# Sliding-window attention as banded dense scores, with a new layout of the projected memory tokens and later weight loads

## Chip, cores and metric

One core of one Trainium2 chip. The metric is the device time of one launch in microseconds (us). Times quoted are medians of several executions; all executions that are compared are in the fast state unless said otherwise (for the 16 runs of the kernel before that ran beside the changed one the record lists no states; the highest is 1.7% above the lowest). Stage times come from one profiled execution of each kernel.

## The reference, cut to what matters

The output is `g * a + (1 - g) * b` for 2048 tokens of width 640. `b` is a sliding attention: each token looks at 8 tokens, 2 apart, with 32 heads of width 20. `a` is a recurrent attention over 64 segments of 32 tokens; 8 memory tokens pass from one segment to the next.

```python
def _B_ref(x, wqkv, wo):
    B, S, D = x.shape
    H = 32
    W, dil = (8, 2)
    ...                                    # q, k, v = x @ wqkv, 32 heads of 20
    idx = pos[:, None] - off[None, :]      # off = 0, 2, 4 .. 14
    mask = idx >= 0
    logits = jnp.einsum('bhsd,bhswd->bhsw', q, kg) * scale
    logits = jnp.where(mask[None, None, :, :], logits, -1000000000.0)
    attn = _softmax(logits, axis=-1)
    o = jnp.einsum('bhsw,bhswd->bhsd', attn, vg)
    return (...) @ wo

def _A_ref(x, mem0, Wq, Wk, Wv, Wo, seg_len):
    for s in range(n_seg):                 # 64 segments, one after the other
        h = jnp.concatenate([mem, xs], axis=1)
        ...                                # q, k, v: 640 -> 32 heads of 192
        ...                                # causal attention within the segment
        o = jnp.einsum('bhte,hed->btd', o, Wo)
        mem = o[:, :M, :].copy()
        outs.append(o[:, M:, :])
```

## The kernel before

It has three stages, one after the other. *Part B* is the sliding attention. The *prepass* projects the last 8 tokens of every segment (512 tokens in all) to queries, keys and values and packs them by segment into a buffer in DRAM. *Part A* is the loop over segments; it reads that buffer and streams 22 of the 80 weight slices (384 KB each) again for each segment, while 58 stay in SBUF.

Part B before (cut): for each of the 8 window positions an elementwise product, summed over each head's 20 rows by a matmul with a 0/1 matrix; then the weights are spread back over the rows by a second 0/1 matmul, copied, multiplied by the shifted values, and summed by identity matmuls.

```python
for w in range(8):
    prod = wk.tile([128, KC, BT], BF, name="prod")
    eng = nc.vector if w % 2 == 0 else nc.gpsimd
    eng.tensor_tensor(out=prod[:], in0=qT[:], in1=kT[:, :, 14 - 2 * w:14 + BT - 2 * w], op=ALU.mult)
    ...                       # 20 head-sum matmuls
...                           # max, exp, sum, reciprocal, product
for c in range(KC):
    for wh in range(2):
        ...                   # 16 expansion matmuls into e_ps
        for sb in range(4):
            nc.scalar.copy(ae[:], e_ps[sb][:])
            eng = nc.vector if ei % 3 != 2 else nc.gpsimd
            eng.tensor_tensor(out=pv[:], in0=ae[:], in1=vwin, op=ALU.mult)
            ...               # 4 identity matmuls into o_ps
```

The prepass before (cut). `evac` copies PSUM to SBUF and takes its engine from a pattern: "a" is ScalarE, "d" is VectorE; here the pattern is "add", so VectorE gets two of three.

```python
k.evac_pat = "add"
...
k.part_b(); k.load_late(0); k.prepass(); k.load_late(1); k.part_a()

with tc.tile_pool(name="pre_zs", bufs=2) as zp:
    zT = zp.tile([128, KC, NZ], BF, name="zT", bufs=1)
    nc.scalar.dma_start(zT[:], self.zT_dram[:].rearrange("p c i s -> p c (i s)"))
    for mi, m in enumerate(("q", "k")):
        for R in range(4):
            ZS = zp.tile([128, nseg, 96], BF, name="ZS")
            sls = [self.get_slice((m, R, kc)) for kc in range(KC)]
            for j in range(4):
                for t in range(3):
                    ...       # 5 matmuls of 128x512 into ps
                    zc = ZS[:].rearrange("p s (c i) -> p i s c", i=8)[:, :, :, 4 * t + j] if m == "q" else \
                        ZS[:].rearrange("p s (i c) -> p i s c", i=8)[:, :, :, 4 * t + j]
                    self.evac(zc, ps[:].rearrange("p (i s) -> p i s", i=8))
            z0 = (768 if m == "q" else 0) + 96 * R
            nc.scalar.dma_start(self.zpk_dram[:, :, z0:z0 + 96].rearrange("s p f -> p s f"), ZS[:])
    ...                       # the value part: 16 groups of 15 matmuls, ZV, stores
```

Of the 58 slices that stay, 29 (values and output weights) are loaded late, 21 after part B and 8 after the prepass, because part B needs the room.

The softmax here doesn't subtract the row's maximum and nothing guards it: scores larger than these inputs give would overflow.

Of the kernel before, what the change touches and what calls it, by code (L numbers as in the profile page):

```python
# [8 lines left out]
ALU = mybir.AluOpType  # L9
# [5 lines left out]
NEG = -1.0e9  # L15

N_STREAM = 22
N_LATE = 29
N_LATE2 = 8
# [9 lines left out]
class _K:  # L29
# [26 lines left out]
    def pst(self, shape, dtype=F32, name="ps"):  # L56
        shape = list(shape)
        assert shape[0] == 128
        nfree = 1
        for d in shape[1:]:  # L60
            nfree *= d
        tot = 2048 // mybir.dt.size(dtype)
        assert nfree <= tot
        t = self.psum.tile([128, tot], dtype, tag="ps", name=name)
        v = t[:, 0:nfree]
        if len(shape) > 2:
            names = "abcdef"[:len(shape) - 1]
            v = v.rearrange("p (%s) -> p %s" % (" ".join(names), " ".join(names)), **dict(zip(names, shape[1:])))
        return v

    def warm(self, n):
        n = int(round(n * _DEV.get("warm", 0)))
        if n <= 0:
            return
        pf = self.pst([128, 128], F32, name="ps_warm")
        for i in range(n):
            self.nc.tensor.matmul(pf[:], lhsT=self.ident[:], rhs=self.ident[:], start=True, stop=True,
                                  skip_group_check=True)
# [21 lines left out]
    def build_consts_b(self, const):  # L100
        nc = self.nc
        ones = const.tile([128, 640], BF, name="ones")
        nc.vector.memset(ones[:], 1.0)
        KC = self.KC
        eh = const.tile([128, KC, 32], BF, name="ehead")
        nc.gpsimd.affine_select(out=eh[:], in_=ones[:, 0:KC * 32].rearrange("p (c h) -> p c h", c=KC),
                                pattern=[[128, KC], [-20, 32]], compare_op=ALU.is_ge, fill=0.0, base=0,
                                channel_multiplier=1)
        nc.gpsimd.affine_select(out=eh[:], in_=eh[:], pattern=[[-128, KC], [20, 32]], compare_op=ALU.is_ge,
                                fill=0.0, base=19, channel_multiplier=-1)  # L110
        self.ehead = eh
        eht = const.tile([128, 640], BF, name="eheadT")
        for sb in range(4):
            sl = slice(32 * sb, 32 * sb + 32)
            nc.gpsimd.affine_select(out=eht[sl, :], in_=ones[sl, :], pattern=[[1, 640]], compare_op=ALU.is_ge,
                                    fill=0.0, base=0, channel_multiplier=-20)
            nc.gpsimd.affine_select(out=eht[sl, :], in_=eht[sl, :], pattern=[[-1, 640]], compare_op=ALU.is_ge,
                                    fill=0.0, base=19, channel_multiplier=20)
        self.eheadT = eht

    def part_b(self):
        nc, tc, KC, S = self.nc, self.tc, self.KC, self.S
        BT = _DEV.get("BT", 512)
        SBT = BT // 4
        NTB = BT // 128
        NB = S // BT
        scale_b = 20.0 ** (-0.5)
        self.bsc_dram = self.dram.tile([S, 640], BF, name="bsc_dram")
        self.zT_dram = self.dram.tile([128, KC, 8, S // 32], BF, name="zT_dram")
# [3 lines left out]
        with ExitStack() as ctx:  # L133
            wpool = ctx.enter_context(tc.tile_pool(name="b_w", bufs=1))
            xin = ctx.enter_context(tc.tile_pool(name="b_xin", bufs=2))
            act = ctx.enter_context(tc.tile_pool(name="b_act", bufs=_DEV.get("b_act_bufs", 1)))
            wk = ctx.enter_context(tc.tile_pool(name="b_wk", bufs=_DEV.get("b_wk_bufs", 2)))
            sm = ctx.enter_context(tc.tile_pool(name="b_sm", bufs=_DEV.get("b_sm_bufs", 1)))
            self.build_consts_b(wpool)
            wqkv_sb = wpool.tile([128, KC, 1920], BF, name="wqkv_sb")  # L140
            nc.scalar.dma_start(wqkv_sb[:], self.wqkv.rearrange("(c p) f -> p c f", p=128))
            wo_sb = wpool.tile([128, KC, 640], BF, name="wo_sb")
            nc.scalar.dma_start(wo_sb[:], self.wo.rearrange("(c p) f -> p c f", p=128))
            gw_sb = wpool.tile([128, KC, 1], BF, name="gw_sb")
            nc.scalar.dma_start(gw_sb[:], self.gate_w.rearrange("(c p o) -> p c o", p=128, o=1))
            gz_sb = wpool.tile([128, self.NT], F32, name="gz_sb")
            halo_k = wpool.tile([128, KC, 14], BF, name="halo_k")
            halo_v = wpool.tile([128, KC, 14], BF, name="halo_v")
            nc.gpsimd.memset(halo_k[:], 0.0)
            nc.gpsimd.memset(halo_v[:], 0.0)  # L150

            for blk in range(NB):
                t0 = blk * BT
                xT = act.tile([128, KC, BT], BF, name="xT_blk")
                xs = []
                for i in range(NTB):
                    x_sb = xin.tile([128, 640], BF, name="x_sb")
                    nc.scalar.dma_start(x_sb[:], self.x2d[t0 + i * 128:t0 + (i + 1) * 128, :])
                    xs.append(x_sb)
                for kc in range(KC):  # L160
                    ps = self.pst([128, BT], BF, name="ps_xT")
                    for i in range(NTB):
                        nc.tensor.transpose(ps[:, i * 128:(i + 1) * 128], xs[i][:, kc * 128:(kc + 1) * 128],
                                            self.ident[:])
                    self.evac(xT[:, kc, :], ps[:])
                nsb = BT // 32
                xv = xT[:].rearrange("p c (s t) -> p s c t", t=32)
                xh = act.tile([128, nsb, KC, 32], BF, name="xh_blk")
                nc.gpsimd.tensor_copy(xh[:, :, :, 8:32], xv[:, :, :, 0:24])
                nc.gpsimd.tensor_copy(xh[:, :, :, 0:8], xv[:, :, :, 24:32])  # L170
                nc.gpsimd.dma_start(self.xh_dram[blk * nsb:(blk + 1) * nsb].rearrange("s p f -> p s f"),
                                    xh[:].rearrange("p s c t -> p s (c t)"))
                zx = act.tile([128, KC, 8, nsb], BF, name="zx_blk")
                nc.gpsimd.tensor_copy(zx[:].rearrange("p c i s -> p s c i"), xv[:, :, :, 24:32])
                nc.gpsimd.dma_start(self.zT_dram[:, :, :, blk * nsb:(blk + 1) * nsb].rearrange("p c i s -> p (c i) s"),
                                    zx[:].rearrange("p c i s -> p (c i) s"))
                ps_g = self.pst([128, NTB], F32, name="ps_g")
                for i in range(NTB):
                    for kc in range(KC):
                        nc.tensor.matmul(ps_g[:, i:i + 1], lhsT=xT[:, kc, i * 128:(i + 1) * 128],  # L180
                                         rhs=gw_sb[:, kc, :], start=(kc == 0), stop=(kc == KC - 1))
                gsl = slice(blk * NTB, (blk + 1) * NTB)
                nc.vector.tensor_copy(gz_sb[:, gsl], ps_g[:])
# [116 lines left out]
    def weights_setup(self):  # L300
# [20 lines left out]
        for k in rest:  # L321
            if k in self.late_keys:
                continue
# [458 lines left out]
```

## Time and profile before

| | before |
|---|---|
| median, all 16 runs beside the changed kernel | 2356.55 us (2335.93 to 2376.16) |
| part B ends, prepass starts (profiled run, span 2353.4) | 427 us |
| prepass: queries and keys / values | 161 / 55 us |
| hand-over to part A | 17 us |
| part A | 1693 us |

The stages are read from when tiles of one stage are first and last touched, and then from the busy time of all engines between those moments. The prediction below prints those rows. In a row the numbers are the stretch, its length, the busy time of each engine with its number of instructions, the granted TensorE clock, the mean busy share of the 16 DMA engines, and GB/s.

### The profile page before, as it was taken

What the parts mean: (1) busy time and instruction counts of PE and PEld (TensorE: products, weight loads), DVE (VectorE), ACT (ScalarE), POOL (GpSimd) and SP (SyncE); (2) the same over time, 40 slices, a digit from 0 to 9 for tenths busy, and PEclk for the clock granted to TensorE, in tenths of its full rate; (3) what the DMA queues carried; (4) which work ended last, traced back from release to release, by engine and by line L of the source; (5) the groups of instructions that cost most, each with busy time, mean ns of one, the idle gap of its engine ahead of it and who ended that gap; (6) DMA issues with size and microseconds to landing.
All of it is one profiled execution on the core that took longest, in us unless ns stands there. A gap on an engine that the chain in (4) does not pass through costs nothing.

```text
span 2353.4 us, 90790 instructions
## 1 busy us (share of the span) xinstructions
PE 1978.4 (84%) x40951; PEld 1135.8 (48%) x40951; DVE 944.9 (40%) x2148; ACT 784.0 (33%) x1807; POOL 211.4 (9%) x196
## 2 busy tenths in 40 slices
PE   3566575776979999999998999999999998899998
PEld 1334243322445555555555555555555555555555
DVE  2554545799423333333333333333333333333333
ACT  0314233455123333333333333333333333333333
POOL 4452544000010000000000000000000000000000
PEclk9575675899989999999999999999999999999999
DMA  8110010677699999999999999999999999999997
GB/s 309 48 40 23 15 32 1 210 101 114 173 326 344 334 326 370 345 365 328 364 333 347 345 348 359 330 363 329 360 341 339 356 344 345 327 358 349 355 343 294
DMA packets 329396, 649.09 MB, mean 276 GB/s; under 512 B 107280, under 2 KB 129744, under 8 KB 329008
## 3 DMA queue, kind: packets, MB, share of 16 engines
q1 hardware_dynamic: 221104, 583.23, 69.4%
q10 hardware_dynamic: 104720, 49.57, 8.8%
q0 software_dynamic: 3184, 10.49, 1.6%
q8 instruction: 320, 5.24, 0.8%
q14 instruction: 68, 0.56, 0.1%
HBM read 615.79 MB, written 29.36 MB: 274 GB/s over the span
## 4 chain that ended last, share of the span: by engine, by line
PE 51%; DMA 23%; DVE 9%; issue 8%; POOL 6%; ACT 3%; ACTq 0%; POOLq 0%; DVEq 0%; SPq 0%
PE ps_qk L490 14%; PE ps_wo L629 8%; DMA wst<-in_A_Wv_dram 7%; PE ps_v L567 6%; DMA wst<-in_A_Wk_dram 6%; DVE ZS L89 6%; PE ps_qkT L504 4%; DMA wst<-wscr 4%; POOL prod L213 3%; PE ps_oT L585 3%; PE ps_woz L629 2%; PE o_ps L259 2%; POOL pv L257 2%; DMA wst<-in_A_Wq_dram 2%; PE ps_S L521 2%
## 5 line engine op out<-in xcount | busy, mean ns | idle before, releaser
L495 ACT CAST QS<-ps_qk 128x384 bf16<-128x384 f32 x512 | 239.8, 479 | 485.8 <-PE ps_qk L490 465.4
L490 PEld LDWEIGHTS <-hT 128*32 128x32 bf16 x10240 | 239.6, 96 | 179.9 <-issue 40.1
L490 PE MATMUL ps_qk<-wst,hT 128*32 128x384 bf16 x2816 | 243.6, 334 | 21.1 <-DMA wst<-in_A_Wk_dram 15.9
L567 PE MATMUL ps_v<-wlate_v,hT 128*32 128x384 bf16 x3584 | 238.9, 331 | 1.3 <-issue 1.2
L629 PEld LDWEIGHTS <-ZQ 128*32 128x32 bf16 x6144 | 187.1, 100 | 109.2 <-issue 47.1
L490 PE MATMUL ps_qk<-wres_k,hT 128*32 128x384 bf16 x3584 | 227.4, 329 | 0.9 <-issue 0.8
L490 PE MATMUL ps_qk<-wres_q,hT 128*32 128x384 bf16 x3840 | 217.8, 331 | 7.5 <-issue 4.1
L504 PE MATMUL ps_qkT<-ident,QS 128*128 128x128 bf16 x1536 | 174.9, 223 | 29.8 <-ACT QS L495 29.8
L598 DVE CAST ZQ<-ps_oT 128x192 bf16<-128x192 f32 x256 | 79.6, 352 | 266.2 <-ACT ZQ L598 266.2
L507 DVE COPY ZQ<-ps_qkT 128x384 bf16<-128x384 bf16 x256 | 91.4, 357 | 212.8 <-PE ps_qkT L504 212.7
L504 PEld LDWEIGHTS <-QS 128*128 128x128 bf16 x1536 | 88.3, 98 | 176.2 <-issue 101.6
L567 PEld LDWEIGHTS <-hT 128*32 128x32 bf16 x5120 | 119.7, 96 | 101.5 <-issue 45.1
L89 DVE CAST ZS<-ps_pre 128x512 bf16<-128x512 f32 x64 | 163.6, 2984 | 9.5 <-PE ps_pre L373 9.5
L629 PE MATMUL ps_wo<-wst,ZQ 128*32 128x384 bf16 (+1 forms) x1408 | 153.0, 328 | 16.6 <-issue 9.2
L511 DVE COPY KV<-ps_qkT 128x384 bf16<-128x384 bf16 x256 | 91.6, 358 | 180.1 <-PE ps_qkT L504 180.1
L629 PE MATMUL ps_wo<-wlate_ob,ZQ 128*32 128x256 bf16 x2688 | 149.2, 285 | 9.2 <-issue 9.2
L567 PE MATMUL ps_v<-wst,hT 128*32 128x384 bf16 x1536 | 134.3, 333 | 24.1 <-DMA wst<-in_A_Wv_dram 21.2
L629 PE MATMUL ps_wo<-wlate_oa,ZQ 128*32 128x384 bf16 x2048 | 150.5, 347 | 4.6 <-issue 4.1
L717 POOL DMA_DIRECT2D out_dram<-a x16 | 8.7, 544 | 1606.6 <-DVE ZQ L507 1412.3
L598 ACT CAST ZQ<-ps_oT 128x192 bf16<-128x192 f32 x256 | 69.2, 322 | 233.6 <-PE ps_oT L592 233.6
L251 ACT CAST ae<-e_ps 128x512 bf16<-128x512 f32 x160 | 88.2, 588 | 74.7 <-PE e_ps L245 45.9
L259 PE MATMUL o_ps<-pv,ident 128*128 128x128 bf16 x640 | 90.0, 300 | 27.3 <-POOL pv L257 17.5
(145 smaller groups left out, 2688.9 us busy)
## 6 DMA issues: line engine op xcount, KB each, us to landing
wst<-in_A_Wk_dram SPq DMA_DIRECT2D x390, 384.0 KB, 5.5
wst<-in_A_Wv_dram SPq DMA_DIRECT2D x390, 384.0 KB, 5.7
wst<-in_A_Wq_dram SPq DMA_DIRECT2D x325, 384.0 KB, 5.6
wst<-wscr SPq DMA_DIRECT2D x320, 384.0 KB, 5.4
ZQ<-zpk_dram ACTq DMA_DIRECT2D x64, 288.0 KB, 5.7
zpk_dram<-ZS ACTq DMA_DIRECT2D x8, 1536.0 KB, 10.7
zpk_dram<-ZV ACTq DMA_DIRECT2D x32, 192.0 KB, 3.1
wres_q<-in_A_Wq_dram SPq DMA_DIRECT2D x15, 384.0 KB, 6.7
```

Of the source, the lines that this page charges most:

```text
L89: nc.vector.tensor_copy(out, in_)
L213: eng.tensor_tensor(out=prod[:], in0=qT[:], in1=kT[:, :, 14 - 2 * w:14 + BT - 2 * w], op=ALU.mult)
L251: nc.scalar.copy(ae[:], e_ps[sb][:])
L259: nc.tensor.matmul(o_ps[:, sb * SBT:(sb + 1) * SBT], lhsT=self.ident[:], rhs=pv[:, wi, :], start=first, stop=(wh == 1 and wi == 3), skip_g ...
L490: nc.tensor.matmul(pq[32 * j:32 * j + 32, 0:384], lhsT=hT[:, kc, :], rhs=sl[:, 384 * j:384 * j + 384], start=(kc == 0), stop=(kc == KC - 1 ...
L495: nc.scalar.copy(st, pq[:, 0:384])
L504: nc.tensor.transpose(pT[:, t, :, :, :].rearrange("p j b i -> p (j b i)"), st[:, 128 * t:128 * t + 128], self.ident[:])
L507: nc.vector.tensor_copy(QT[:, 1:5, 12 * R:12 * R + 12, :].rearrange("p b c i -> p c b i"), pT.rearrange("p t j b i -> p (t j) b i"))
L511: nc.vector.tensor_copy(KT[:, 12 * R:12 * R + 12, :].rearrange("p c k -> p (c k)"), pT.rearrange("p t j b i -> p (t j b i)"))
L567: nc.tensor.matmul(pv[32 * j:32 * j + 32, 0:384], lhsT=hT[:, kc, :], rhs=sl[:, 384 * j:384 * j + 384], start=(kc == 0), stop=(kc == KC - 1 ...
L598: cp(oTx[:, c0:c0 + 6, :], pos[j // 2][:, j % 2, 0:240].rearrange("p (c q) -> p c q", q=40)[:, :, 8:40])
L629: nc.tensor.matmul(pss[part][32 * jj:32 * jj + 32, 0:n], lhsT=oT[:, 24 * (R // 2) + 6 * j + 3 * (R % 2) + t, :], rhs=o_weights(part, c), s ...
```

## The change

The intent is to turn part B into dense matmuls, to make the prepass's scattered stores cheap, and to give part B the room for this by loading most weights after it. Four parts:

1. **Part B.** Even and odd tokens are two sequences, so the window is a band of 8 in each. Heads are padded from 20 to 32 rows. For each block of 484 tokens and group of 4 heads there are dense scores (128 keys by 121 queries), two exps and two products with a band mask (one for each pair of heads), value matmuls and ones matmuls for the sums, and 1/sum as exp(-ln).
2. **Late loads.** 55 of the 58 slices that stay are loaded late: 46 after part B (12 query, 14 key, 14 value, 6 output), 9 after the prepass.
3. **Layout.** In the prepass the segment is now the outer and the position in it the inner index. The query store writes runs of 8 bf16; the key store still steps 24 bytes per element.
4. **Split.** Evictions alternate between the two engines ("ad").

```diff
-N_LATE = 29
-N_LATE2 = 8
+N_LATE = 55
+N_LATE2 = 9
 ... part B rewritten (cut to the inner step)
+            def scores(b, g):
+                ...
+                for hp in range(2):
+                    ps = psS.tile([128, 2, 512], F32, tag="S", name="ps_bS")
+                    for u in range(nu):
+                        a = 242 * (u // 2) + u % 2
+                        for r in range(2):
+                            rs = slice(64 * hp + 32 * r, 64 * hp + 32 * r + 32)
+                            nc.tensor.matmul(ps[0:nk, r, nq * u:nq * u + nq], lhsT=kT[rs, a:a + 2 * nk - 1:2],
+                                             rhs=qT[rs, a:a + 2 * nq - 1:2], ...)
+                    nc.scalar.activation(Pv, ps[0:nk, :, 0:nq * nu], ACT.Exp, scale=scale_b)
+                    nc.vector.tensor_tensor(out=P4, in0=P4, in1=m.to_broadcast([nk, 2, nu, nq]), op=ALU.mult)
+            def values(b, g):
+                ...           # ones and value matmuls into pz and po, one bank each
+                nc.scalar.activation(rz[:, 0:nt], pz[:, 0:nt], ACT.Ln)
+                nc.scalar.activation(rz[:, 0:nt], rz[:, 0:nt], ACT.Exp, scale=-1.0)
+                nc.vector.tensor_tensor(out=dst, in0=po..., in1=rz..., op=ALU.mult)
 ... order of a step: next projection, scores, values of the step before, output tile
 ... late loads
-        self.late_keys = set(cand[len(cand) - N_LATE:])
+        first = ["q", "k", "v", "oa", "ob"]
+        self.late = sorted(rest, key=lambda k: first.index(k[0]))[-N_LATE:]
 ... prepass
-                            zc = ZS[:].rearrange("p s (c i) -> p i s c", i=8)[:, :, :, 4 * t + j] if m == "q" else \
-                                ZS[:].rearrange("p s (i c) -> p i s c", i=8)[:, :, :, 4 * t + j]
-                            self.evac(zc, ps[:].rearrange("p (i s) -> p i s", i=8))
+                            zc = ZS[:].rearrange("p s (c i) -> p s c i", i=8)[:, :, 4 * t + j, :] if m == "q" else \
+                                ZS[:].rearrange("p s (i c) -> p s c i", i=8)[:, :, 4 * t + j, :]
+                            self.evac(zc, ps[:].rearrange("p (s i) -> p s i", i=8))
 ... value stores: 4 instead of 2 per tile, half of them issued by GpSimd
-    k.evac_pat = "add"
+    k.evac_pat = "ad"
```

## The prediction

> **What bounds the kernel now.** The program has three stages that run one after the other: the sliding-window attention (part B), the projection of the segment-end tokens (the prepass), and the 64 segments of the recurrent attention (part A). I first asked for the lifetimes of the tiles that mark the borders. The first prepass matmul starts at 427 us, the last scattered-layout eviction ends near 590, the last prepass matmul near 643, and part A runs steadily from 660. Then I read the busy time of every engine in those stretches.
>
> ```profile
> core 0: us, PE busy (x) PEld busy (x) DVE busy (x) ACT busy (x) POOL busy (x), PEclk, DMA share, GB/s
> 0.00:37.00 37.00, 2.82 (x23) 2.01 (x23) 1.43 (x5) 2.07 (x3) 11.21 (x24) 1.00 0.92 340
> 130.00:226.00 96.00, 60.55 (x622) 35.59 (x620) 49.22 (x61) 30.51 (x55) 44.75 (x27) 0.63 0.10 22
> 421.00:427.00 6.00, 0.00 (x0) 0.00 (x0) 0.00 (x0) 0.00 (x0) 0.00 (x0) 0.74 0.69 243
> 427.00:588.00 161.00, 121.10 (x481) 49.08 (x482) 158.34 (x63) 84.73 (x32) 0.00 (x0) 0.92 0.75 144
> 588.00:643.00 55.00, 53.46 (x239) 23.57 (x238) 24.84 (x34) 8.90 (x16) 0.00 (x0) 0.97 0.63 165
> 643.00:660.00 17.00, 2.07 (x43) 1.21 (x43) 1.74 (x25) 1.43 (x3) 7.03 (x40) 0.68 0.83 247
> 660.00:2353.40 1693.40, 1554.18 (x37651) 916.76 (x37648) 560.61 (x1774) 562.75 (x1534) 16.93 (x32) 0.98 0.96 344
> ```
>
> The reader sees three things. One block of part B takes 96 us with no engine over 61 us busy and the matmul clock at 0.63: it is a chain of waits, not a full engine. The query and key half of the prepass takes 161 us with VectorE busy 158 of them. Part A takes 1693 us with DMA at 0.96 and PE at 0.92, and the change leaves it alone. So 72% of the span is out of reach.
>
> Next, the groups of part B and of the prepass, to name the links.
>
> ```profile
> L213 DVE TENSOR_TENSOR prod<-qT_blk,kT_ext x16: 1492/3838/5596, 51.6 to 356.5; 128x2560 bf16<-128x2560 bf16 x16
> L213 POOL TENSOR_TENSOR prod<-qT_blk,kT_ext x16: 4597/4874/5907, 53.2 to 361.1; 128x2560 bf16<-128x2560 bf16 x16
> L257 DVE TENSOR_TENSOR pv<-ae,vT_ext x108: 413/426/1317, 87.5 to 414.0; 128x512 bf16<-128x512 bf16 x108
> L87 ACT CAST qT_blk<-ps_qkv x7: 586/586/587, 41.8 to 336.3; 128x512 bf16<-128x512 f32 x7
> L89 DVE CAST kT_ext<-ps_qkv x14: 690/691/693, 46.1 to 341.6; 128x512 bf16<-128x512 f32 x14
> L89 DVE CAST ZS<-ps_pre x64: 2718/2984/3019, 429.7 to 590.3; 128x512 bf16<-128x512 f32 x64
> L87 ACT CAST ZS<-ps_pre x32: 2707/2726/3132, 432.3 to 584.4; 128x512 bf16<-128x512 f32 x32
> ```
>
> Columns after the colon are least, median and largest nanoseconds. The products of line 213 take turns on VectorE and GpSimd, 5 us apiece when they meet. The prepass eviction of 128x512 costs VectorE 2984 ns where the plain one costs 691, and ScalarE 2726 where the plain one costs 586: the same data, scattered into ZS.
>
> **What the Trainium skill says.** (1) "TensorE: Matmul & The Clock Gate", Part 1: an idle window of about 3.4 us brings the array to half rate. The trace agrees: 0.63 granted in part B's block with its 4 to 9 us gaps, 0.97 in the dense 588 to 643. (2) "SBUF — State Buffer", Door 1: lines of 16 bytes, and each access to a new line is penalised. The trace agrees: the scattered store steps 192 bytes per element and costs four times the plain one, while the query transposes' copy in part A, in runs of 8 bf16, takes the 358 ns of the contiguous key copy. (3) "VectorE: DVE Perf Modes", the tier table: tensor_tensor in bf16 has a double rate, and single with a PSUM operand. The trace agrees: 2560 elements in 1492 ns at best is 1.7 per ns. (4) "ScalarE: Activation LUTs", What ACT_TABLE_LOAD costs: 0.833 ns per element for every function; here 586 ns for 512 and 479 for 384 give 0.84 and a fixed 0.16 us. Exp and Ln share one loaded table, as before.
>
> **The change, part by part.**
>
> *Part B is rewritten.* It removes all elementwise products over eight window positions, the head-sum matmuls, the max, the head-expansion matmuls with their 160 ScalarE copies, and the identity-matmul sums. In their place even and odd tokens are separate sequences, in which the dilated window is a band of 8; per block of 484 tokens and group of 4 heads the kernel makes dense scores of 128 keys by 121 queries, one exp, a band mask, a value matmul and a ones matmul for the sums. There are 32 full steps (4 blocks, 8 groups) and 8 short ones of 112 tokens.
>
> PE per full step: projections are 10 matmuls of 484 and 498 columns. The old 128x512 matmul runs at 0.216 us in a stream (five in 1.08), so 10 x 0.207 = 2.07 us. Scores: 16 of 121 columns, two row tiles at once; the old expansion matmuls of 128 columns followed each other every 22 ns with four tiles, I take 30, so 0.5. Values and sums: 32 matmuls, the old head-sum ones did 20 in 0.46, so 0.6. Each change of tile shape left 0.2 us of idle before; three give 0.6. Sum 3.8, times 32 is 121. Short steps: 8 x 1.8 = 14. Output tiles: 16 x 16 matmuls of 320 columns at 0.135 = 34. Values projection: 18 x 10 x 0.135 = 24. Transposes and gate: 4 x 2 = 8. PE total 201 us at full clock.
>
> ScalarE per full step: key eviction 0.575, two exps over 968 elements 2 x 0.97, Ln 0.56, Exp 0.60: 3.7, times 32 is 118. Short steps 10, its half of the value, transpose and output evictions 21: 149. VectorE: query eviction 0.66, final product from PSUM 0.66, two masks at 0.65 (double rate) to 1.16 (single): 2.6 to 3.6, so 84 to 116, plus about 35 of the rest: 120 to 150. GpSimd nearly leaves the path.
>
> So PE bounds part B. It won't be full: the projection, value, transpose and output groups share two PSUM banks, and ScalarE's in-order queue puts an eviction behind exps of 1 us. I add about 15% for this: 230. Before the first projection, x, the weights (3.3 MB at some 310 GB/s) and the padded copies take about 15 us, where the old kernel had its first projection at 37. Part B thus ends near 245 instead of 421: minus 176.
>
> *Weights.* Only 3 resident slices now load during part B, and 55 late: 46 after it, 9 after the prepass (21 and 8 before). 46 x 393 KB at 344 GB/s is 53 us, but they arrive in order of use, and five slices feed 13 us of matmuls, while their load takes 5.7. Three of the first five are already there and one is streamed. I keep 4 us of gap for the 6 before: minus 2.
>
> *Prepass.* With the segment outside and the position inside, the query store writes runs of 8 bf16 (16 bytes), so it falls to the plain 0.6 to 0.7 us and PE bounds it: 240 x 0.216 = 52, say 54. The key store still steps 24 bytes per element, a new line each time. I keep the old cost of about 2.6 us, but shared equally by two engines now: 24 x 2.7 = 65. The value half is PE-bound at 55; its stores double in number and half go to GpSimd's queue: 58. Sum 177 instead of 216: minus 39.
>
> *Part A.* Same slices streamed, same code; one more late slice, 1.1 us. The 17 us hand-over stays: stores land, masks are built. Plus 1.
>
> Sum: -176 - 2 - 39 + 1 = -216. From the 2346.85 us median this is 2131; I say 2130.
>
> **The rivals.** *PE-bound as above* is my main one. *Latency chain:* the sums and outputs have one PSUM bank each, so value matmuls, Ln, Exp, product and the next value matmuls are a cycle of about 0.6 + 0.6 + 0.6 + 0.7 plus hand-offs, 3 us; below PE's 6 us per step, but ScalarE's queue can stretch it. If it leads to gaps over 3.4 us the clock drops as it did before, and PE's 201 becomes 300: the end would be near 2200. For it: in-order ScalarE with 3.7 us of fixed work per step. Against: the next projection is issued before each score, so PE has work. *Late weights:* freed buffers come at the very end of part B, so the first prepass matmuls could wait for a queue of 17 MB; if order of use breaks, 20 to 40 us. Against: the order is sorted. *Key store as cheap as the query store* (24-byte steps gentler than 192): the prepass drops by 11 to 165 and the total to about 2118. *Part A slower* because of another buffer layout: nothing in the profile speaks for it.
>
> **Range and chances.** Part B's end between 215 and 300 and the prepass between 163 and 195, not both at the same extreme, give 2085 to 2190. Even the clock-drop rival stays 6% below before, and nothing removed comes back. Faster by over 2%: 0.97, within 2%: 0.02, slower: 0.01.
>
> **What would show it.** By stage: first prepass matmul near 250 us, last near 425, part A about 1690 us at DMA 0.96. In part B the granted clock above 0.85, PE near 80% busy, ScalarE near 60%. Query ZS evictions near 0.7 us, key ones 2.5 to 3. A part B longer than 300 us, with PE idle on ScalarE evictions and a low clock, would prove the second rival; a long DMA wait at the first prepass matmul the third; a part A off by over 15 us would break the assumption on which everything rests.

## The result, and the profile after

The changed kernel takes 2119.78 us (median of 11 runs, 2100.09 to 2123.46) against 2356.55. The ratio is 0.8988, with a 95% interval of 0.8957 to 0.9018. Ratios here are the mean time of one kernel's fast runs over that of the other's of the same rounds, so they are not quite the ratio of the medians quoted. The forecast was 2130.

The busy time of every engine by stage, for the changed kernel, columns as in the prediction's first fence:

```profile
core 0: us, PE busy (x) PEld busy (x) DVE busy (x) ACT busy (x) POOL busy (x), PEclk, DMA share, GB/s
0.00:25.00 25.00, 10.73 (x80) 7.34 (x81) 9.79 (x18) 4.50 (x8) 18.85 (x22) 1.00 0.88 269
25.00:220.30 195.30, 180.09 (x2647) 105.83 (x2645) 111.77 (x208) 134.26 (x241) 20.74 (x38) 1.00 0.21 64
220.30:278.40 58.10, 54.50 (x240) 24.04 (x241) 15.42 (x23) 13.58 (x24) 0.00 (x0) 0.94 1.16 271
278.40:343.40 65.00, 54.29 (x241) 23.66 (x240) 52.60 (x24) 50.16 (x22) 0.00 (x0) 0.95 1.09 246
343.40:401.60 58.20, 53.74 (x241) 23.79 (x240) 17.92 (x24) 18.78 (x26) 15.83 (x30) 0.97 0.67 173
401.60:419.00 17.40, 2.35 (x44) 1.11 (x43) 2.22 (x25) 1.54 (x3) 7.95 (x42) 0.74 0.99 299
419.00:2110.10 1691.10, 1555.04 (x37651) 914.79 (x37649) 560.37 (x1774) 562.68 (x1534) 17.06 (x32) 0.98 0.97 345
```

The rows are: start to the first query or key projection, the rest of part B, the query half, the key half, the value part, the hand-over, part A. Set against before and against the forecast:

| stage, us | before | forecast | after |
|---|---|---|---|
| start to first projection | 37 | 15 | 25.0 |
| first prepass matmul | 427.2 | 249 | 220.3 |
| query half | 161 for both halves | 54 | 58.1 |
| key half | | 65 | 65.0 |
| value part | 55 | 58 | 58.2 |
| hand-over | 17 | 17 | 17.4 |
| part A | 1693.4 | 1694 | 1691.1 |

Part B is now a full engine: PE is busy 180 of 195 us, at a granted clock of 1.00. In the row of before's part B that the prediction shows, no engine had over 61 of 96 us and the clock was 0.63. The new load of PE, by groups of matmuls in the stretch from 25 to 220 us (busy time, mean ns of one, idle time before and what ended it):

```profile
L219 PE MATMUL ps_bqk<-xT,wk_pad 128*128 128x498 bf16 x160 | 38.8, 372 | 0.0
L275 PE MATMUL ps_bo<-wo_pad,OT 128*128 128x320 bf16 x256 | 38.7, 300 | 0.7 <-DVE bqT L75 0.7
...
L259 PE MATMUL ps_bO<-bP,bV 128*32 128x121 bf16 x512 | 18.4, 217 | 5.4 <-DVE OT L267 5.2
...
L237 PE MATMUL ps_bS<-bqT,bkT 32*128 32x121 bf16 x512 | 16.6, 217 | 0.5 <-ACT bP L242 0.5
```

The largest wait in these rows is 5.2 us in all, on the final product (`OT`) of the step before. The feared chain over the single output bank exists, but ends few waits.

The two elementwise operations of a step, from the tile of exponentials (least, median and largest ns; first and last start):

```profile
L242 ACT ACTIVATE bP<-ps_bS x80: 335/982/1007, 29.9 to 216.7; 128x968 bf16<-128x968 f32 x64, 63x224 bf16<-63x224 f32 x16
L246 DVE TENSOR_TENSOR bP<-bP,band x80: 245/666/1619, 30.9 to 217.1; 128x968 bf16<-128x968 bf16 x64, 63x224 bf16<-63x224 bf16 x16
```

The mask product takes 666 ns for 968 elements, the better end of the forecast's 0.65 to 1.16. The exp takes 982 ns where 0.97 us was forecast.

The start is longer than forecast. The matmul timeline of the changed kernel (start, length, instruction, and in brackets the idle time before and what ended it) shows what PE waited for and what it did first:

```profile
5.59 1.01 PE L160 MATMUL ps_xT<-ident,x_sb 128*128 128x128 bf16 x8 [5.59 <-POOL ident L83]
...
13.70 1.01 PE L160 MATMUL ps_xT<-ident,x_sb 128*128 128x128 bf16 x8 [6.26 <-DVE xT L75]
...
22.20 2.94 PE L206 MATMUL ps_bv<-wv_sb,xT 128*128 128x320 bf16 x20 [0.47 <-DVE bV L75]
```

The identity matrix came at 5.6 us. The longest wait, 6.26 us, is for a copy of transposed `x` on VectorE, which until 13.2 us was making padded weight copies that stood ahead of it in its queue. These copies were done near 14.5 us, as the forecast had it. What comes on top is 1.7 us for the gate's weights and the values projection, which the program puts ahead of the first query projection: it fills 17 to 25 us.

In the prepass the query evictions are plain now. The packed tile ZS of the changed kernel: its evictions, what its engines waited for, and how long its stores took:

```profile
L73 ACT CAST ZS<-ps_pre x48: 586/1530/3197, 225.6 to 346.7; 128x512 bf16<-128x512 f32 x48
L75 DVE CAST ZS<-ps_pre x48: 678/1570/3048, 225.9 to 344.3; 128x512 bf16<-128x512 f32 x48
...
  DMA zpk_dram<-ZS: 48.1, 4
...
DMA to landing us min/median/max: 11.7/12.4/31.3
```

The least time, 586 and 678 ns, is the query store; the median mixes it with the key store. What is new is the third line: four waits, 48 us in all, for a *store* of ZS to land, which took up to 31.3 us. Before, the same view had its longest store at 12.4 us and no such wait. The ScalarE timeline shows where:

```profile
260.08 7.23 ACTq L408 DMA_DIRECT2D zpk_dram<-ZS  x1
270.72 2.05 ACT L73 CAST ZS<-ps_pre 128x512 bf16<-128x512 f32 x4 [11.90 <-DMA zpk_dram<-ZS]
...
291.44 14.10 ACT L73 CAST ZS<-ps_pre 128x512 bf16<-128x512 f32 x6 [13.30 <-DMA zpk_dram<-ZS]
```

Twice, near 260 and 280 us, the evictions stand for 12 to 13 us until a store lands and one of the two ZS buffers is free. The last row also gives the key store's price: six evictions back to back in 14.10 us, so 2.35 us each. At the same time SyncE issues the late loads, 384 KB each:

```profile
227.63 22.63 SPq L372 DMA_DIRECT2D wlate_k<-in_A_Wk_dram  x14
250.49 32.61 SPq L372 DMA_DIRECT2D wlate_v<-in_A_Wv_dram  x14
```

Issuing a store was itself held up: the one at 260.08 kept ScalarE for 7.23 us, where the median is 0.37, and the next went out at 288.05, some 8.7 us after the last eviction into its tile. So it is not only the landing that is late.

So the key half had the forecast length, 65.0 us, but two candidates for its cause: the slow evictions that the prediction named (VectorE busy 52.6 of 65), and stores held up by the late loads. This was the question for the experiments, together with part B's true bound.

### The profile page after: what moved, and what is told of

It is laid out like the page before. It is cut to its first block, busy times and chain, and to the rows that moved or that the text cites. A ratio compares the mean times of both kernels' runs of the same rounds, so it can differ in the third digit from the quotient of the medians.

```text
span 2110.1 us, 90993 instructions
## 1 busy us (share of the span) xinstructions
PE 1910.7 (91%) x41135; PEld 1100.6 (52%) x41135; DVE 770.1 (36%) x2095; ACT 785.5 (37%) x1857; POOL 80.4 (4%) x163
## 4 chain that ended last, share of the span: by engine, by line
PE 58%; DMA 25%; issue 8%; ACT 6%; DVE 2%; ACTq 0%; POOL 0%; SPq 0%; POOLq 0%; DVEq 0%
PE ps_qk L518 15%; DMA wst<-in_A_Wv_dram 9%; PE ps_wo L657 8%; PE ps_v L595 7%; DMA wst<-in_A_Wk_dram 5%; DMA wst<-wscr 4%; PE ps_qkT L532 4%; DMA wst<-in_A_Wq_dram 4%; PE ps_oT L613 4%; PE ps_pre L402 3%; PE ps_woz L657 3%; PE ps_bqk L219 2%; ACT bP L242 2%; PE ps_pre L416 2%; PE ps_S L549 2%
## 5 line engine op out<-in xcount | busy, mean ns | idle before, releaser
L657 PEld LDWEIGHTS <-ZQ 128*32 128x32 bf16 x6144 | 182.0, 99 | 108.8 <-issue 43.0
L518 PE MATMUL ps_qk<-wlate_k,hT 128*32 128x384 bf16 x3584 | 229.6, 331 | 8.7 <-issue 8.7
L532 PE MATMUL ps_qkT<-ident,QS 128*128 128x128 bf16 x1536 | 175.7, 224 | 29.4 <-ACT QS L523 29.3
L518 PE MATMUL ps_qk<-wlate_q,hT 128*32 128x384 bf16 x3072 | 173.5, 331 | 0.0
L657 PE MATMUL ps_wo<-wst,ZQ 128*32 128x384 bf16 (+1 forms) x1408 | 150.0, 326 | 13.2 <-issue 6.5
L539 DVE COPY KV<-ps_qkT 128x384 bf16<-128x384 bf16 x256 | 91.6, 358 | 182.9 <-PE ps_qkT L532 182.9
L613 PEld LDWEIGHTS <-KV 32*128 32x128 bf16 (+1 forms) x4096 | 74.4, 96 | 63.3 <-issue 43.8
L669 DVE CAST hT<-ps_mem 128x24 bf16<-128x24 f32 x126 | 22.5, 179 | 221.6 <-PE ps_mem L666 221.6
L549 PE MATMUL ps_S<-ZQ,KV 128*32 128x40 bf16 (+1 forms) x4096 | 95.3, 187 | 1.2 <-issue 1.2
L601 DVE CAST KV<-ps_v 128x384 bf16<-128x384 f32 x128 | 71.0, 555 | 68.9 <-PE ps_v L595 68.9
## 6 DMA issues: line engine op xcount, KB each, us to landing
zpk_dram<-ZS ACTq DMA_DIRECT2D x8, 1536.0 KB, 12.4
```

The source lines that it names most:

```text
L518: nc.tensor.matmul(pq[32 * j:32 * j + 32, 0:384], lhsT=hT[:, kc, :], rhs=sl[:, 384 * j:384 * j + 384], start=(kc == 0), stop=(kc == KC - 1 ...
L532: nc.tensor.transpose(pT[:, t, :, :, :].rearrange("p j b i -> p (j b i)"), st[:, 128 * t:128 * t + 128], self.ident[:])
L539: nc.vector.tensor_copy(KT[:, 12 * R:12 * R + 12, :].rearrange("p c k -> p (c k)"), pT.rearrange("p t j b i -> p (t j b i)"))
L549: nc.tensor.matmul(pSs[h][32 * j:32 * j + 32, par, 40 * r:40 * r + 40], lhsT=KT[k0:k1, c, :], rhs=QT[k0:k1, :, c, :], start=(r == 0 and t ...
L601: nc.vector.tensor_copy(V[:, R, :], pv[:, 0:384])
L613: nc.tensor.matmul(po[j][p0:p0 + f1 - f0, r, t, :], lhsT=V[ks, 2 * h + r, f0:f1], rhs=E[ks, par, 40 * r:40 * r + 40], start=(r == 0 and t ...
```

## The experiments

All compare with the kernel before, run in the same rounds on the same chip. Stage times of the same part B code scatter: the runs that leave part B alone start their prepass between 219.6 and 223.3 us.

### before_even_split: the split alone, in the kernel before

```diff
         k.load_late(0)
+        k.evac_pat = "ad"
         k.prepass()
```

> The kernel before, with the prepass evictions alternating evenly between ScalarE and VectorE (before: one in three on ScalarE), nothing else changed. If each scattered eviction keeps its 2.6 to 2.7 us (theory: the store's step sets the cost, the split sets who pays), the query and key half of the prepass goes from 161 us to 48 x 2.6 to 2.7 = 125 to 130, about 31 us less in all, ratio near 0.987. If the layout alone brought the prepass gain (rival), the half stays above 150 us.

Measured: 2326.6 us (4 runs), ratio 0.9882, interval 0.9822 to 0.9941. The row of the query and key halves:

```profile
430.90:554.90 124.00, 110.60 (x470) 48.16 (x481) 119.21 (x47) 116.12 (x46) 0.00 (x0) 0.95 0.90 175
```

Both eviction engines are busy 116 to 119 of 124 us: still bound by evictions, but now shared, and 37 us shorter than the 161 of before. The value part took 58.2. This is what the working of "half each" gives.

### before_even_layout: split and layout, in the kernel before

The edit adds the change's ZS stores, its `zT` layout and its value stores to the split; weights stay as before (21 late slices ahead of the prepass).

```diff
+        k.evac_pat = "ad"
-                            zc = ZS[:].rearrange("p s (c i) -> p i s c", i=8)[:, :, :, 4 * t + j] if m == "q" else \
-                                ZS[:].rearrange("p s (i c) -> p i s c", i=8)[:, :, :, 4 * t + j]
+                            zc = ZS[:].rearrange("p s (c i) -> p s c i", i=8)[:, :, 4 * t + j, :] if m == "q" else \
+                                ZS[:].rearrange("p s (i c) -> p s c i", i=8)[:, :, 4 * t + j, :]
 ... zx_blk, zT and the ZV stores as in the change
```

> The kernel before with the whole prepass of the change (segment outside, position inside, even split), but the old part B and the old weight loading. Theory: query half 54, key half 65, value part 55 to 58: prepass about 177 instead of 216, so about 39 us less than before, ratio near 0.983; against the run with the even split alone the layout is worth only about 8 us. Rival (layout is the main thing): 20 us or more less than the even split alone.

Measured: 2304.93 us (4 runs), ratio 0.9802, interval 0.9765 to 0.9839. The rows of query half, key half and value part:

```profile
429.30:483.00 53.70, 53.23 (x235) 23.93 (x241) 15.90 (x23) 14.04 (x24) 0.00 (x0) 0.96 1.21 259
483.00:537.30 54.30, 51.94 (x237) 23.38 (x240) 52.48 (x24) 50.30 (x22) 0.00 (x0) 1.00 0.90 146
537.50:595.70 58.20, 53.21 (x236) 23.73 (x239) 17.88 (x24) 18.60 (x26) 15.86 (x30) 0.97 0.67 172
```

and the stores of ZS there:

```profile
DMA to landing us min/median/max: 8.6/12.4/13.6
```

This is the run that overturned my reason. The key half takes 54.3 us, not 65, although its evictions are the same as in the changed kernel (VectorE 52.48 busy here, 52.60 there). PE is busy 51.94 of 54.3: the key half is bound by PE, with two eviction engines just keeping up. No store takes over 13.6 us here. What differs is 25 late slices fewer ahead of the prepass. The start differs too: here PE stood 8.4 us before its first prepass matmul (0.65 in the change), and in 421 to 429 us some 200 GB/s were moved, about four slices, so part of the queue was gone when the prepass began.

### after_old_layout: the changed kernel with the old layout

```diff
-                            zc = ZS[:].rearrange("p s (c i) -> p s c i", i=8)[:, :, 4 * t + j, :] if m == "q" else \
-                                ZS[:].rearrange("p s (i c) -> p s c i", i=8)[:, :, 4 * t + j, :]
+                            zc = ZS[:].rearrange("p s (c i) -> p i s c", i=8)[:, :, :, 4 * t + j] if m == "q" else \
+                                ZS[:].rearrange("p s (i c) -> p i s c", i=8)[:, :, :, 4 * t + j]
 ... zx_blk, zT and the ZV stores as in the kernel before
```

> The changed kernel with the old order of the segment-end tokens (position outside, segment inside) in prepass, its transfers and stores; even split kept. Theory: query half from 58 to about 63 to 65, key half about 63 to 65, value part 55 to 58: 0 to 8 us longer than the changed kernel. Rival (layout is the main thing): 30 us or more longer.

Measured: 2136.72 us (4 runs), ratio 0.9082, interval 0.9044 to 0.9120, against 0.8988 for the change. Query half 67.1, key half 66.5, value part 56.5: 190.1 in all against 181.3. So in the changed kernel the layout is worth about 9 us of prepass, where it was worth 16 in before_even_layout (124.0 to 108.0). The total is 17 us above the change's, where 0 to 8 were expected. This prepass also started late, at 227.6 us, outside the scatter. The trace shows one wait of that size inside part B: ScalarE stood 5.5 us around the issue of the load of `zT` (138.81 us), and PE then 4.4 us. That load reads `zT_dram`, whose stores, in the old layout again, took 9.2 us to landing (median) against 5.7 in the change. That the one caused the other is argued.

### before_late55: a run that did not do what its name says

```diff
-N_LATE = 29
-N_LATE2 = 8
+N_LATE = 55
+N_LATE2 = 9
```

> The kernel before with 55 late slices (46 after part B, 9 after the prepass) in place of 29 (21 and 8), nothing else. Prediction's theory: loads arrive in order of use, 0 to 5 us longer. Rival (the long queue of loads costs): 46 loads hold the DMA engines for some 55 us, so the scattered stores wait behind them and the query half stalls: 8 to 15 us longer. The strong rival of the prediction: 20 to 40 us longer.

Measured: 2363.7 us (4 runs), ratio 1.0033, interval 0.9986 to 1.0080. The prepass started at 435.6 us and took 157.6 and 58.4, and no store took over 12.6 us. The list of transfers shows that the test was void:

```profile
wlate_v<-in_A_Wv_dram SPq DMA_DIRECT2D x11, 384.0 KB, 6.4
...
wres_v<-in_A_Wv_dram SPq DMA_DIRECT2D x3, 384.0 KB, 4.9
```

Only 26 slices were late, three fewer than before, and three value slices joined the resident ones. The kernel before chooses late slices from the 29 value and output slices only, by `cand[len(cand) - N_LATE:]`; with 55 the index is -26, and Python takes the last 26. The run says nothing on 46 late loads.

### scores_twice: every score matmul of part B done twice

The second pass left the result as it was.

```diff
-                    for u in range(nu):
+                    for u in list(range(nu)) * 2:
```

> The changed kernel with every score matmul of part B issued twice (same result): 0.43 us more PE work per full step. If PE bounds part B: 32 x 0.43 + 8 x 0.3, about 16 us longer in part B (195 to 211), PE busy stays above 90%. If ScalarE's in-order queue bounds it (rival): under 4 us.

### ln_twice: the logarithm of the sums done twice

```diff
                 nc.scalar.activation(rz[:, 0:nt], pz[:, 0:nt], ACT.Ln)
+                nc.scalar.activation(rz[:, 0:nt], pz[:, 0:nt], ACT.Ln)
```

> The changed kernel with the Ln of part B computed twice (same result): 0.59 us more ScalarE work per full step, 32 x 0.55 + 8 x 0.25, about 20 us in sum. If PE bounds part B: under 5 us longer. If ScalarE's queue bounds it (rival): 15 to 20 us longer.

The two ask part B's question: PE bound, or bound by the chain sums, Ln, Exp, product, next values. Part B after its first projection, first of scores_twice, then of ln_twice:

```profile
25.00:238.70 213.70, 196.83 (x3217) 121.45 (x3215) 112.85 (x208) 138.26 (x240) 20.74 (x38) 0.98 0.20 59
```

```profile
25.00:233.80 208.80, 185.37 (x2648) 106.86 (x2647) 113.09 (x209) 152.48 (x281) 20.30 (x38) 0.98 0.20 61
```

Scores_twice adds 16.7 us of PE work (196.83 less 180.09) and ends part B at 238.7, some 15 to 19 us after the 219.6 to 223.3 of unchanged part Bs: all of it reaches the end, as PE-bound says. Ln_twice adds 18.2 us of ScalarE work (152.48 less 134.26) and ends at 233.8, 10 to 14 us later: neither theory in pure form. If PE alone were the bound, little of it would have shown. Most steps are held by PE, but steps that carry no output tile or values projection have less PE work, and there the chain shows even in the changed kernel, as in this step of its matmul timeline:

```profile
107.15 0.24 PE L259 MATMUL ps_bZ<-bP,b_ones 128*32 128x121 bf16 x4
108.08 0.24 PE L259 MATMUL ps_bO<-bP,bV 128*32 128x121 bf16 x4 [0.69 <-DVE OT L267]
```

The value matmuls stood 0.69 us until the final product of the step before had read the one output bank. An extra Ln lengthens that wait; that this makes up the whole 10 to 14 us was not taken apart further. The totals were 2122.03 us (ratio 0.9016, 0.8965 to 0.9066) and 2123.02 (0.9021, 0.8960 to 0.9083); the intervals include the change's own ratio.

### key_runs_wrong: the key store as cheap as the query store

The key rows are written in runs of 8 like the query rows, and part A still reads them the old way: the result is wrong.

```diff
-                            zc = ZS[:].rearrange("p s (c i) -> p s c i", i=8)[:, :, 4 * t + j, :] if m == "q" else \
-                                ZS[:].rearrange("p s (i c) -> p s c i", i=8)[:, :, 4 * t + j, :]
+                            zc = ZS[:].rearrange("p s (c i) -> p s c i", i=8)[:, :, 4 * t + j, :]
```

> The changed kernel with the key store in runs of 8 bf16 like the query store; the reader is not changed, so the result is wrong on purpose (the matmul that reads the keys takes a stationary operand with one step only). If the 24-byte step is the cost: key evictions 0.6 to 0.7 us, the half PE-bound after the wait for its buffer, key half from 65 to 54 to 58, total 7 to 10 us less. If something else (cast, bank hand-over) makes key evictions slow: no change.

Measured: 2105.08 us (4 runs), ratio 0.8941, interval 0.8897 to 0.8985. The evictions and then the rows of the key half and the value part:

```profile
L75 DVE CAST ZS<-ps_pre x48: 680/691/693, 228.0 to 346.2; 128x512 bf16<-128x512 f32 x48
```

```profile
278.90:345.80 66.90, 55.74 (x241) 24.28 (x240) 16.32 (x24) 13.78 (x24) 0.00 (x0) 0.90 1.14 250
345.80:397.60 51.80, 51.80 (x242) 23.44 (x240) 15.25 (x24) 12.69 (x23) 15.90 (x30) 1.00 0.72 190
```

Every eviction is plain now (at most 693 ns on VectorE), VectorE is busy 16.3 us, and the key half still takes 66.9. The slow stepped eviction is thus not what sets it: the waits on landing stores are, 49.6 us here (48.1 in the change). The gain of about 6 us was expected in the key half; it came in the value part, 51.8 instead of 58.2. A likely reason, argued and not shown: in the change the last key store goes out 6.1 us into the value part, and there ScalarE stood 7.4 us to issue the first value stores and VectorE 10.2 us until one landed; here the last key store goes out after 1.1 us, and these waits are 6.5 and 4.5 us.

Two warnings. The wrong result passed the comparison: presumably the 8 memory keys weigh too little for its tolerance. Whatever the reason, the comparison does not guard this buffer. And the right version of this store was not to be had: reading keys in runs of 8 needs two free steps in the stationary operand of part A's score matmul, and the build refused a second one ("exactly one free dimension").

### late_v_after_k: the value and output slices later

The 20 late value and output slices are issued behind the last streamed key slice.

```diff
+            if part == 0 and k[0] in ("v", "oa"):
+                ...
+                self.held.append((v, src))
 ... at the end of the key half
+            with tc.issue_after(self.last_load.ins):
+                for v, src in self.held:
+                    nc.sync.dma_start(v[:], src)
```

> The changed kernel with the 20 late value and output slices loaded behind the last streamed key slice in place of at once. If these loads hold up the store of the query tiles (31 us to landing against 12): stores land in 12 to 15 us, the waits for the store buffer (48 us on two engines) go, query half 58 to about 53 to 55, key half 65 to about 57 to 60, total 7 to 12 us less. Rival (store itself slow, or the value slices then come too late): no gain, or the value part grows.

Measured: 2107.76 us (4 runs), ratio 0.8974, interval 0.8909 to 0.9040. Query half 57.0, key half 63.3, value part 55.4; stores landed in 18.0 us at most, waits on them 42.3 us. The longest store is shorter, but the key half only by 2 us, which is inside the scatter: three executions with the change's own prepass (the change, scores_twice, ln_twice) have 65.0 to 68.6. The jam moved rather than went.

### spread_loads: the same, in portions through the value part

Each row group of value slices is released when the group before it starts.

```diff
+            def release(n):
+                with tc.issue_after(self.last_load.ins):
+                    for v, src in self.held[:n]:
+                        nc.sync.dma_start(v[:], src)
+                del self.held[:n]
             for R in range(4):
                 sls = [self.get_slice(("v", R, kc)) for kc in range(KC)]
+                release(nv[R + 1] if R < 3 else len(self.held))
```

> The changed kernel with the late value slices of each quarter loaded one quarter ahead of use, from the last key loads on, and the six late output slices after the value part's loads. Theory (the queue of late loads holds up the stores of the query tiles): from 280 us on the transfers have room, stores land in under 18 us, key half from 65 to 56 to 60 us, value part 55 to 58, total 5 to 10 us less than the changed kernel. Rival (the 24 query and key slices, loaded at once, are what holds up the stores): key half stays above 62 us, as with the loads merely moved behind the keys (63).

Measured: 2120.8 us (6 runs), ratio 0.8988, interval 0.8951 to 0.9025: the change's own ratio. Query half, key half, value part:

```profile
222.50:279.00 56.50, 53.26 (x235) 23.91 (x241) 15.42 (x23) 13.58 (x24) 0.00 (x0) 0.97 1.16 271
279.00:336.90 57.90, 53.73 (x237) 23.80 (x241) 53.32 (x24) 51.03 (x22) 0.00 (x0) 0.97 1.05 232
336.90:405.40 68.50, 54.05 (x237) 23.82 (x239) 18.12 (x25) 18.25 (x27) 15.86 (x30) 0.90 0.79 192
```

Together with key_runs_wrong this settles the key half: with the slow evictions kept and the loads moved away it takes 57.9 us, against 65.0 to 68.6 in the three executions of the unchanged prepass. But the value part grew from 58.2 to 68.5, by as much as was won, and the whole prepass is no shorter.

### three_store_buffers: three ZS buffers

The room for the third comes from two more slices loaded after the prepass.

```diff
-N_LATE2 = 9
+N_LATE2 = 11
-                    ZS = zp.tile([128, nseg, 96], BF, name="ZS")
+                    ZS = zp.tile([128, nseg, 96], BF, name="ZS", bufs=3)
```

> The changed kernel with three buffers for the store tile of the prepass in place of two (two more output slices wait for the end of the prepass), the loads as they were. If the wait for the buffer is what the late loads cost: the evictions run on while a store is slow, query and key half 123 to 108 to 114 us, total 8 to 14 us less. Rival (the streamed key slices behind the queue of late loads set the key half): under 4 us less, and the matmuls wait on the streamed slices near 300 us.

Measured: 2120.34 us (6 runs), ratio 0.8997, interval 0.8961 to 0.9033. Query half 51.8, key half 70.3, value part 58.9. The waits on landing stores are gone and the query half is at PE's pace. But the key half then waited for weights (9.1 us of PE's idle time for a streamed key slice alone). ScalarE stood 16.3 us until 290.3, put down to a late value slice, around the issue of the next store: a third buffer alone does not free a store from the queue of loads. The rival, that matmuls then wait for streamed slices, came true. Again no net gain.

### spread_and_three, and spread_three_masks

The first joins the two edits. The second also builds part A's masks from another tile, so that they need not wait for the end of the prepass:

```diff
-            self.build_sel(pers, QS[:, 0:160])
+            self.build_sel(pers, oTz[:].rearrange("p c q -> p (c q)")[:, 0:160])
-tc.tile_pool(name="a_pers", bufs=1)
+tc.tile_pool(name="a_pers", bufs=1, reuse_waits="tile")
```

> Both: loads spread and three store buffers. Theory: query and key half at the 108 us that the old kernel with the new prepass had, value part 52 to 58, total 13 to 20 us less than the changed kernel, near 2100. Rival: no more than the better of the two alone.

> As before, and the constants of the recurrent part built from a tile that no early eviction waits for, with its buffers freed one by one: the hand-over from the last prepass matmul to the first transposed query, 17 us in both kernels, drops by the 7 us of mask building, perhaps by part of the 8 us wait for the last stores. Total 20 to 30 us less than the changed kernel. Rival: the hand-over is set by the value stores' landing or by the late output slices, and at most 2 us go.

Measured: spread_and_three 2113.85 us (6 runs), ratio 0.8961, interval 0.8933 to 0.8989; query half 51.3, key half 60.5, value part 67.0. Spread_three_masks 2107.99 us (6 runs, one of them slow and left out of the ratio), ratio 0.8937, interval 0.8901 to 0.8972; 51.8, 60.2 and 66.7. Its point value is the best of all right kernels, half a per cent below the change's 0.8988 (0.8957 to 0.9018), but the intervals overlap, so I don't call it shown. From the end of the prepass to part A's first transposed queries it took 21.5 us against 23.7 in spread_and_three: 2 us less. The change itself has 17.3 there, spread_loads 17.0, but three_store_buffers 24.2. The traces show why: in the three runs with three buffers the first segment's input `hT` is loaded only after the prepass (issued at 407 to 412 us), and PE stands 14.9 to 15.5 us for it. In the change and spread_loads it is loaded near 40 us, and there PE waits 14.0 and 14.2 us for ScalarE's query copies, which wait for the masks. So the mask edit was tried only where another wait held the hand-over; what it is worth in the change was not tested. Part A then ran 1681 to 1683 us in the three runs with three buffers, against 1691 in the change, so that from the end of the prepass to the end of the kernel there are 1704 to 1709 us in all four.

### What the prepass runs say together

The last column is the sum over the three stages of DMA share times length, from rows like those above: the busy time of an average DMA engine in the prepass.

| run | query | key | value | sum | DMA share x time |
|---|---|---|---|---|---|
| before_even_layout (21 late loads ahead) | 53.7 | 54.3 | 58.2 | 166.2 | 153 |
| change (46) | 58.1 | 65.0 | 58.2 | 181.3 | 177 |
| scores_twice (46) | 54.5 | 68.6 | 58.4 | 181.5 | 175 |
| ln_twice (46) | 55.1 | 67.7 | 57.9 | 180.7 | 176 |
| late_v_after_k (46, moved) | 57.0 | 63.3 | 55.4 | 175.7 | 177 |
| key_runs_wrong (46) | 56.6 | 66.9 | 51.8 | 175.3 | 179 |
| spread_loads (46, moved) | 56.5 | 57.9 | 68.5 | 182.9 | 180 |
| three_store_buffers (44) | 51.8 | 70.3 | 58.9 | 181.0 | 176 |
| spread_and_three (44, moved) | 51.3 | 60.5 | 67.0 | 178.8 | 176 |
| spread_three_masks (44, moved) | 51.8 | 60.2 | 66.7 | 178.7 | 176 |

The rows of scores_twice and ln_twice have the change's own prepass, so they show the scatter: 54.5 to 58.1, 65.0 to 68.6 and 57.9 to 58.4, while the sum holds to 180.7 to 181.5. In every run of the changed kernel in this table the DMA engines have 175 to 180 us of work in a prepass of 175 to 183 us. In before_even_layout they have 153 in 166, and PE paces it. The 25 more slices are 9.8 MB, which at part A's 345 GB/s is an estimated 28 us of transfer; the DMA column grew by 24, and the bytes moved (GB/s times length) from 31.8 to 41.8 MB. So my reading is that the queue of late loads makes DMA as full as PE: edits that move loads or add buffers choose *where* PE waits, not how long. What is shown is that the sum hardly moved. That transfer time is the cause is argued from the column, since its share counts overlaps, is no strict limit, and in the value part is only 0.67 in the change: DMA is not full throughout; a changed kernel with 20 late loads fewer would settle it. It was not built, as part B's buffers take the room of these slices.

A page may bear on why the stores suffer most, though no run here varies the size of their pieces. The Trainium skill, "DMA: Bandwidth & Descriptors", Specifications, gives 512 bytes as the least transfer for line rate; ZS is stored in pieces of 192 bytes (96 bf16). In the kernel before, such a store of 1536 KB took 10.7 us to landing (median), so 147 GB/s, beside some loads, where part A's loads run at 345; behind the late loads it took up to 31.3 us.

## Why the prediction was right

The forecast of 2130 us missed the median by 10 us. Its direction and the size of its main term were right; several errors cancelled in part. Some of the closeness is luck of the base: the forecast started from 2346.85 us, the median of four earlier runs, while the kernel before took 2356.55 beside the change. It foretold 216 us less, and 237 were measured, 21 more.

- **Part B becomes PE-bound: right.** PE 180 of 195 us busy at clock 1.00; doubling the scores lengthened it by all that was added. Only in the main, though: an Ln more on ScalarE cost 10 to 14 us. PE's own sum was forecast at 201; measured, 180 after the first projection and 11 before, so 191.
- **The stall term was mis-sized.** "I add about 15% for this: 230." Measured, 195 us with 180 busy, so 15 us of stalls in place of 29. The other 21 of the 35 us are PE's sum: 10 less work in all, and 11 done before the first projection.
- **The start was mis-sized the other way.** Forecast 15, measured 25.0: the weights and padded copies were there at about 14.5 as forecast, but the gate's weights and above all the values projection, 17 to 25 us, come before the first query projection. The sum had this projection's work, but not its place. Together, part B ends 25 us sooner than the 245 forecast.
- **Late weights: the step that failed.** The prediction had them "arrive in order of use" and kept 4 us of gap, "minus 2". The gap was indeed nil (first prepass matmul at 220.3). But it asked only whether the weights come in time, not what their queue does to other transfers. In the changed kernel the prepass is 181.3 us, in before_even_layout 166.2: 15 us longer, with the queue as the argued cause. About 7 of them are net, as before_even_layout paid 8.4 us of gap first (174.6 with the gap, 182.0 in the change). That gap and prepass came out near the forecast (182 for 181) is luck: split and layout gave 50 us (216 to 166.2) where 39 was forecast, and the late loads took 15 back where nothing was.
- **Key half: right number, wrong reason.** "I keep the old cost of about 2.6 us ... 24 x 2.7 = 65." The eviction costs 2.35 us; alone it would give 24 x 2.35 = 56, hardly over PE's pace, and before_even_layout shows 54.3. Key_runs_wrong keeps 66.9 us without any slow eviction, and spread_loads has 57.9 with all of them. The 65.0 (up to 68.6 in other executions) is the store jam.
- **Query half and value part:** 58.1 for 54, 58.2 for 58. The 4 us of the first have the jam as a likely cause, but the same prepass ran its query half in 54.5 and 55.1 in scores_twice and ln_twice, so they are within scatter. Of the second, 6 us go when the key store is cheap (51.8 in key_runs_wrong), where the prediction had added 3 for the value stores.
- **Split and layout:** worth 37 us (161 to 124.0) and 16 us (to 108.0) in queries and keys; the late loads took back 15 (to 123.1).
- **Hand-over and part A: right.** 17.4 for 17; 1691.1 for 1694. The assumption on which everything rested held.
- **Rivals.** The clock drop is refuted (1.00 for 0.63 before). The latency chain is there in part: an Ln more cost 10 to 14 us. The prediction set the chain's 3 us against "PE's 6 us per step", which is all of PE's 201 us over 32 steps; by its own sum a step without output tile or values projection has 3.8, hardly more than the chain. The late-weights rival named what is the likely cause, but at the wrong place: no long wait at the first matmul, but stores of ZS that landed up to 19 us later than the median of 12.4.

In sum, by stages: 29 us sooner at the first prepass matmul, 4 us longer in the prepass (181.3 for 177), 3 us shorter in part A, so 27 us under a forecast that reads 2137 for the profiled run (2353.4 less 216); it took 2110.1.

## What to carry to other kernels

When a kernel turns elementwise windows into dense banded matmuls, dense work on an engine kept busy can take half the time of elementwise work handed between engines: here 195 us against 384 (37 to 421). When loads are moved, ask not only whether they arrive in time but which other transfers then stand in their queue, above all stores whose buffer is waited for. And a forecast that hits its number is not yet understood: take the suspected cost away and see whether the stage shortens, and count in the trace that the edit did what it says.

## What the Trainium skill lacked or had wrong

- "SBUF — State Buffer", which the prediction cites for its 16-byte lines, gives no cost for 2-byte results scattered over lines. The runs show, for 512 elements from PSUM: 2.35 us at a step of 24 bytes on ScalarE and 2.7 to 3.0 at 192 bytes, against 0.59 (ScalarE) and 0.69 (VectorE) in runs of 16 bytes.
- "VectorE: DVE Perf Modes", Mode 2×_1P, asks for 4-byte alignment for the double rate, without saying of what. Here the mask product has rows of 121 bf16 (242 bytes), so every other row inside the operand lies off 4 bytes, with the mask repeated for every row, and still takes 666 ns for 968 elements, 1.45 per ns: it was enough here that the tile starts aligned.
- "DMA: Bandwidth & Descriptors" has no figure for a store in 192-byte pieces beside a full load queue. Here 1.5 MB took 10.7 us (median) before and up to 31.3 us beside 46 loads of 384 KB.
- "TensorEngine Tiling (Array Packing)", Key Properties, says that a change of tiling mode drains TensorE, and gives no figure. In the list of waits of the changed kernel, the weight loads ahead of the row-tiled scores stood 13.2 us in 33 places, 0.40 each, with nothing that the profile shows them to wait for; PE itself stood only 0.5 us ahead of those scores. That the drain is the reason is not shown.
